# Loading the whole Toeplitz strip of a convolution from HBM in place of half of it

## The chip, the cores and the metric

The kernel runs on one core of a Trainium2 chip. The metric is the device time of one execution in microseconds (us), lower is better. All runs compared here are fast-state runs, each against runs of the kernel before on the same chip and in the same rounds. Experiments of different rounds are compared by their medians; the kernel before had medians of 2366.5 to 2369.3 us in all rounds. The Trainium skill, which is cited by page title below, is a set of notes on the chip; where a number below is not attributed to it, it comes from a run or a trace.

## The reference

```python
def _attn_ref(x, h) -> np.ndarray:       # x: (8, 5696, 128), h: (5696, 128), float32
    B, S, D = x.shape
    L = 2 * S
    Xf = np.fft.rfft(x, n=L, axis=1)
    Hf = np.fft.rfft(h, n=L, axis=0)
    Yf = Xf * Hf[None, :, :]
    y = np.fft.irfft(Yf, n=L, axis=1)[:, :S, :]
    return y.astype(np.float32)
# ... cut: a token- and channel-mixing layer on y follows, unchanged here
```

The first stage is a causal convolution along the sequence, with its own filter for each of the 128 channels.

## The kernel before

The convolution is done as matrix products. The sequence is cut into NT = 45 blocks of P = 128, and for channel `d` and block distance `k` TensorE needs the 128 x 128 Toeplitz block whose row p is the padded filter `h_pad[d]`, shifted by p elements. A *strip* holds KS = 15 such blocks side by side; its row p is 1920 neighbouring elements of `h_pad[d]`, starting at `j0 + p`. A channel takes three strips and 45 matmuls, which get narrower as `k` grows.

```python
x_sb2 = x_sb.rearrange("q d t b -> q d (t b)")
with tc.tile_pool(name="conv_sbuf", bufs=6) as csb, \
     tc.tile_pool(name="conv_psum", bufs=2, space=bass.MemoryType.PSUM) as cps:
    for d in range(D):
        psum = cps.tile([P, NT * B], F32, tag="convps")
        for k0 in range(0, NT, KS):
            k1 = k0 + KS
            w = KS * P
            j0 = P * k0
            strip = csb.tile([P, KS * P + 64], BF16, tag="strip")

            own, other, c0, c1 = ((slice(0, 64), slice(64, P), 0, 64) if d % 2 == 0 else
                                  (slice(64, P), slice(0, 64), 64, 0))
            nc.sync.dma_start(strip[own, :w + 64],
                              bass.AP(tensor=h_pad.tensor, offset=h_pad.offset + d * HW + j0,
                                      ap=[[1, 64], [1, w + 64]]))
            nc.vector.tensor_copy(strip[other, c0:c0 + w], strip[own, c1:c1 + w])
            for k in range(k0, k1):
                ntj = NT - k
                c = c0 + (k - k0) * P
                nc.tensor.matmul(psum[:, B * k: B * k + B * ntj],
                                 strip[:, c:c + P],
                                 x_sb2[:, d, :B * ntj],
                                 start=(k == 0), stop=(k == NT - 1))
        nc.scalar.activation(
            y_sb[:, :, :, d].rearrange("q t b -> q (t b)"), psum, AF.Copy)
# ... the mixing layer follows
```

Row p + 64 of a strip is row p shifted by 64 elements. So the DMA brings only 64 rows, 64 elements longer than needed, and VectorE copies them, shifted, into the other 64 partitions. Six buffers hold the strips, exactly two channels' worth.

Of the kernel before, what the change touches and what calls it, by code (L numbers as in the profile page):

```python
# [21 lines left out]
def kernel(  # L22
# [10 lines left out]
    nc = tc.nc  # L33
    B, S, D = x.shape
    assert D == 128
    P = 128
# [3 lines left out]
    HW = Sp + P  # L40
    KS = 15
# [12 lines left out]
    h_pad = h_pad_h.ap()  # L54
# [26 lines left out]
    with tc.tile_pool(name="s0", bufs=1, side="right") as s0, \  # L81
# [27 lines left out]
        for tj in range(NT):  # L109
            q_cnt = P if tj < NT - 1 else S_last  # L110
            tmp = xl.tile([P, B, D], F32, tag="xt")
            if q_cnt < P:
# [3 lines left out]
                                      ap=[[D, q_cnt], [S * D, B], [1, D]]))  # L116
# [22 lines left out]
# [7 lines that stand above are left out]
                j0 = P * k0  # L146
                strip = csb.tile([P, KS * P + 64], BF16, tag="strip")

                own, other, c0, c1 = ((slice(0, 64), slice(64, P), 0, 64) if d % 2 == 0 else
                                      (slice(64, P), slice(0, 64), 64, 0))  # L150
                nc.sync.dma_start(strip[own, :w + 64],
                                  bass.AP(tensor=h_pad.tensor, offset=h_pad.offset + d * HW + j0,
                                          ap=[[1, 64], [1, w + 64]]))
                nc.vector.tensor_copy(strip[other, c0:c0 + w], strip[own, c1:c1 + w])  # L154
                for k in range(k0, k1):
                    ntj = NT - k
                    c = c0 + (k - k0) * P
# [6 lines that stand above are left out]
# [148 lines left out]
    with tc.tile_pool(name="bpool", bufs=1, reuse_waits="tile") as bp, \  # L312
# [155 lines left out]
        for k, (p, tt, c) in enumerate(chunks):  # L468
            j0, nj = CHUNKS[c]
# [55 lines left out]
        for i, (k, p, tt, j0, s0, nj) in enumerate(stretches):  # L525
# [20 lines left out]
            if tt is None:  # L546
# [17 lines left out]
                if end_of_pair:  # L564
# [5 lines left out]
                    for h in range(2):  # L570
                        c, c0 = cs[h]
# [87 lines left out]
```

## Time and profile before

| | kernel before |
|---|---|
| time, median of 2 runs | 2368.76 us (2365.74 to 2371.78) |
| span of the profiled execution | 2367.9 us |
| convolution: first to last weight load | 106.7 to 597.9 us |
| a strip's DMA, issue to landing, median | 4.6 us |

The first view is that of one tile, `strip`, in the kernel before. The rows with a line number give an instruction group with its shortest, median and longest duration in ns and the first and last start in us. The indented rows with a tile's name say what ended the idle time of the engines that work on the tile (us in total, times); an indented `PEld` row comes from the view's second list, who waited for the tile, and is that of TensorE's weight loads alone.

```profile
L158 PEld LDWEIGHTS <-strip x5760: 95/98/152, 106.7 to 597.9; 128*128 128x128 bf16 x199
...
L151 SPq DMA_DIRECT2D strip<-h_pad x384: 444/445/1586, 100.8 to 590.4; - x192
L154 DVE COPY strip<-strip x384: 651/655/658, 106.0 to 595.3; 64x1920 bf16<-64x1920 bf16 x192
...
  DMA strip<-h_pad: 205.1, 309
  DVE strip L154: 36.8, 75
...
  PEld L158: 21.2, 41
...
DMA to landing us min/median/max: 3.3/4.6/7.2
```

The last weight load starts at 597.9 and the first at 106.7, so a strip takes (597.9 - 106.7) / 384 = 1.279 us. VectorE waits for strips (205 us), and TensorE waits for VectorE's copies.

The second is the view by stretches, of the kernel before, for 460 us within the convolution: the stretch and its length, busy us (and instructions) of TensorE, its weight loads, VectorE, ScalarE and GpSimd, then the granted clock, the busy share of the 16 DMA engines, and GB/s.

```profile
core 0: us, PE busy (x) PEld busy (x) DVE busy (x) ACT busy (x) POOL busy (x), PEclk, DMA share, GB/s
110.00:570.00 460.00, 445.47 (x5424) 382.55 (x5422) 235.10 (x361) 213.23 (x120) 0.00 (x0) 1.00 0.76 200
```

TensorE is busy 445 of 460 us at full clock, while the DMA engines are busy 76% at 200 GB/s. The third is the chain of waits of the kernel before, in order of time (start, us, what), a piece of the convolution.

```profile
215.71 5.75 PE psum L158 x60
...
221.48 5.27 DMA strip<-h_pad
...
226.87 0.67 DVE strip L154
...
227.58 13.09 PE psum L158 x150
...
240.68 4.76 DMA strip<-h_pad
```

Where TensorE waits for nothing it does 60 matmuls, four strips, in 5.75 us: a channel's three and the first and widest of the next channel, which takes 2.12 us. The three strips of a channel thus take 3.63 us, or 1.21 us a strip. Between such stretches the chain runs through a strip's DMA (about 5 us) and a copy (0.67 us).

### The profile page before, as it was taken

How to read it: one execution, taken by the hardware profiler on the slowest of the kernel's cores; microseconds unless marked ns; L12 is line 12 of the kernel's file. 1: busy time of each engine (PE TensorE's matmuls, PEld its weight loads, DVE VectorE, ACT ScalarE, POOL GpSimd, SP SyncE). 2: the span in 40 equal slices, each digit the busy share in tenths (PEclk: the TensorE clock that was granted, in tenths of full speed). 3: DMA queues.
4: the chain of work that ended last, by engine and by line, in shares of the span. 5: the costliest groups of instructions: out<-in, count | busy, mean ns of one | idle time of the engine just before them, and what ended most of it. 6: DMA issues, size and time to landing. Idle time of an engine off the chain costs nothing.

```text
span 2367.9 us, 39718 instructions
## 1 busy us (share of the span) xinstructions
PE 2191.0 (93%) x14513; PEld 1216.4 (51%) x14686; DVE 1649.6 (70%) x2997; ACT 639.2 (27%) x733; POOL 796.1 (34%) x1474
## 2 busy tenths in 40 slices
PE   4699999999666999999999999799999999999997
PEld 1188888888432444444444444234444444444443
DVE  5655555555577888887787776687677677677774
ACT  3544444444862333332232000001111111111111
POOL 0000000000201544544446564344544544544540
PEclk7599999999978999999999999899999999999998
DMA  9977777777998988988789997967877977977872
GB/s 238 251 204 203 200 204 202 202 197 202 232 284 218 164 156 168 164 165 156 134 168 164 159 151 128 286 101 134 156 136 130 160 134 134 160 132 136 151 135 54
DMA packets 435332, 405.51 MB, mean 171 GB/s; under 512 B 66497, under 2 KB 370625, under 8 KB 435009
## 3 DMA queue, kind: packets, MB, share of 16 engines
q0 software_dynamic: 222816, 131.33, 42.4%
q1 hardware_dynamic: 209296, 260.55, 38.9%
q10 hardware_dynamic: 3024, 11.08, 1.3%
q8 instruction: 116, 1.90, 0.3%
q14 instruction: 80, 0.65, 0.1%
HBM read 449.27 MB, written 84.75 MB: 226 GB/s over the span
## 4 chain that ended last, share of the span: by engine, by line
PE 70%; DMA 15%; DVE 8%; issue 3%; POOL 2%; ACT 1%; SPq 1%; DVEq 0%; ACTq 0%; POOLq 0%
PE m L598 51%; PE psum L158 14%; DMA strip<-h_pad 6%; DMA tmp<-in_x_dram 2%; DVE c L605 2%; POOL wb L326 2%; DMA wb<-in_moe_w_tok_r_dram 2%; DMA wb<-in_moe_w_tok_i_dram 2%; DMA h_bf<-in_h_dram 1%; DVE wt L335 1%; DVE strip L154 1%; PE v L419 1%; PE utp L412 1%; PE m L560 1%; PE m L562 1%
## 5 line engine op out<-in xcount | busy, mean ns | idle before, releaser
L326 POOL DMA_DIRECT2D wb<-in_moe_w_tok_i_dram x720 | 388.7, 547 | 801.7 <-DVE wt L335 713.8
L326 POOL DMA_DIRECT2D wb<-in_moe_w_tok_r_dram x720 | 387.6, 546 | 714.4 <-PE psum L158 594.3
L158 PE MATMUL psum<-x_sb,strip 128*128 128x360 bf16 (+44 forms) x5760 | 474.1, 243 | 17.0 <-DVE strip L154 15.2
L598 PE MATMUL m<-b,wt 128*128 128x512 bf16 x1892 | 453.7, 383 | 26.9 <-DVE wt L335 9.8
L158 PEld LDWEIGHTS <-strip 128*128 128x128 bf16 x5760 | 406.5, 98 | 85.4 <-DVE strip L154 21.2
L335 DVE STREAM_TRANSPOSE wt<-wb 128x384 f32<-128x384 f32 (+2 forms) x720 | 359.8, 524 | 123.1 <-PE m L598 73.5
L154 DVE COPY strip<-strip 64x1920 bf16<-64x1920 bf16 x384 | 250.7, 655 | 239.3 <-DMA strip<-h_pad 205.1
L598 PEld LDWEIGHTS <-wt 128*128 128x128 bf16 x1936 | 190.6, 99 | 259.8 <-issue 27.6
L162 ACT ACTIVATE y_sb<-psum 128x360 bf16<-128x360 f32 x128 | 227.4, 1777 | 264.4 <-PE psum L158 264.4
L605 DVE TENSOR_TENSOR c<-c,m 128x512 f32<-128x512 f32 x440 | 284.0, 671 | 0.0
L414 ACT ACTIVATE uts<-utp 128x512 bf16<-128x512 bf16 (+1 forms) x90 | 53.3, 592 | 616.7 <-PE utp L412 616.7
L409 ACT ACTIVATE ub<-c 128x512 bf16<-128x512 f32 (+1 forms) x90 | 56.5, 628 | 226.6 <-DVE c L605 226.3
L121 PE MATMUL rps<-tmpbf,R_bf 128*128 128x512 bf16 x88 | 45.7, 620 | 52.1 <-DVE tmpbf L118 52.0
L185 ACT ACTIVATE yT<-tpz 128x512 bf16<-128x512 bf16 x68 | 39.7, 596 | 191.5 <-PE tpz L181 191.5
L118 DVE CAST tmpbf<-tmp 128x1024 bf16<-128x1024 f32 x45 | 56.7, 1267 | 33.3 <-DMA tmp<-in_x_dram 33.1
L199 ACT ACTIVATE red<-theta_ps,magic 128x512 f32<-128x512 f32 x46 | 31.6, 687 | 151.3 <-PE theta_ps L197 116.9
L421 DVE SCALAR_TENSOR_TENSOR c<-v,c 128x512 f32<-128x512 f32 (+1 forms) x90 | 61.6, 684 | 11.3 <-PE v L419 10.8
L123 ACT ACTIVATE x_sb<-rps 128x1024 bf16<-128x1024 f32 x45 | 46.1, 1024 | 57.8 <-PE rps L121 50.1
L219 ACT ACTIVATE mag<-mag,half_pi 128x512 f32<-128x512 f32 (+1 forms) x68 | 57.8, 850 | 0.2
L605 DVE TENSOR_TENSOR c<-yy,m 128x512 f32<-128x512 bf16 x88 | 56.1, 679 | 0.9 <-PE m L598 0.9
L121 PEld LDWEIGHTS <-R_bf 128*128 128x128 bf16 x90 | 6.2, 111 | 89.5 <-DVE tmpbf L118 80.8
L217 ACT ACTIVATE mag<-red 128x512 f32<-128x512 f32 x46 | 29.0, 630 | 77.6 <-DVE red L201 77.6
(2759 smaller groups left out, 2967.7 us busy)
## 6 DMA issues: line engine op xcount, KB each, us to landing
strip<-h_pad SPq DMA_DIRECT2D x384, 248.0 KB, 4.6
wb<-in_moe_w_tok_r_dram POOLq DMA_DIRECT2D x352, 96.0 KB, 4.4
wb<-in_moe_w_tok_i_dram POOLq DMA_DIRECT2D x352, 96.0 KB, 4.6
wb<-in_moe_w_tok_r_dram POOLq DMA_DIRECT2D x352, 80.0 KB, 4.3
wb<-in_moe_w_tok_i_dram POOLq DMA_DIRECT2D x352, 80.0 KB, 3.7
tmp<-in_x_dram SPq DMA_DIRECT2D x44, 512.0 KB, 5.8
cp_hbm<-c SPq DMA_DIRECT2D x88, 256.0 KB, 2.5
c<-cp_hbm SPq DMA_DIRECT2D x88, 256.0 KB, 4.6
```

The lines of the kernel that those rows point to most:

```text
L118: nc.vector.tensor_copy(tmpbf, tmp.transpose([0, 2, 1]))
L154: nc.vector.tensor_copy(strip[other, c0:c0 + w], strip[own, c1:c1 + w])
L158: nc.tensor.matmul(psum[:, B * k: B * k + B * ntj], strip[:, c:c + P], x_sb2[:, d, :B * ntj], start=(k == 0), stop=(k == NT - 1))
L162: nc.scalar.activation(y_sb[:, :, :, d].rearrange("q t b -> q (t b)"), psum, AF.Copy)
L219: nc.scalar.activation(mag, mag, AF.Sin, bias=half_pi, scale=-TWO_PI)
L326: nc.gpsimd.dma_start(wb[32 * i:32 * i + 32, :ng, :nj * 64], bass.AP(tensor=a.tensor, offset=a.offset + row0 * S + p * H + i * QR + j0 * 6 ...
L335: nc.vector.transpose(wt.rearrange("p j t r -> p (j t r)").bitcast(F32).rearrange("p (j g t) -> p g j t", j=TJ, g=4)[:, :ng, :nj], wb[:, : ...
L409: nc.scalar.activation(ub[:m].rearrange("p b d -> p (b d)"), c[:m], AF.Copy)
L414: nc.scalar.activation(uts[:, :, :m], utp[:, :, :m], AF.Copy)
L421: nc.vector.scalar_tensor_tensor(c[:m], v[:m], 0.0, c[:m], op0=ALU.max, op1=ALU.add)
L598: nc.tensor.matmul(ms[q], a[q][:, j, :, r], bts[jj][q][:, r, :], start=(jj == 0 and r == 0), stop=(jj == NJ - 1 and r == 1 and q not in left))
L605: nc.vector.tensor_tensor(c, z, ms[q], op=op)
```

## The change

The intent is to free VectorE and to take its copy out of the way between DMA and TensorE: the DMA brings all 128 rows, and to carry twice the DMA work the strips are issued in turn on the sync and the scalar queue.

```diff
-                own, other, c0, c1 = ((slice(0, 64), slice(64, P), 0, 64) if d % 2 == 0 else
-                                      (slice(64, P), slice(0, 64), 64, 0))
-                nc.sync.dma_start(strip[own, :w + 64],
-                                  bass.AP(tensor=h_pad.tensor, offset=h_pad.offset + d * HW + j0,
-                                          ap=[[1, 64], [1, w + 64]]))
-                nc.vector.tensor_copy(strip[other, c0:c0 + w], strip[own, c1:c1 + w])
+                eng = nc.sync if (d * 3 + k0 // KS) % 2 == 0 else nc.scalar
+                c0 = 0
+                eng.dma_start(strip[:, :w],
+                              bass.AP(tensor=h_pad.tensor, offset=h_pad.offset + d * HW + j0,
+                                      ap=[[1, P], [1, w]]))
```

The number of buffers, six, and their width stay.

## The prediction

> **What bounds the kernel now.** The change touches only the convolution (106 to 598 us of a 2368 us span). By stretches, TensorE is busy 57 to 58.7 of every 60 us there at granted clock 1.00; the chain of waits shows one channel's three strips, back to back, in 3.63 us, so 128 channels need at least 465 us. About 490 pass. The other 25 us are waits: by the wait view TensorE sits idle 36 us for VectorE's half-strip copy (74 times), and VectorE 205 us for the strip's DMA (309 times). The chain alternates: TensorE frees a buffer, a strip lands about 5 us later, 0.66 us of copy, TensorE again. The stage is close to TensorE-bound; a loop of six buffers and slow strips just shows through. DMA is 73 to 78% busy, moving only 200 GB/s.
>
> **Why the strips are slow.** A strip fills 64 partitions. The Trainium skill, "SBUF — State Buffer", section "Door 1", says that partitions 0 to 63 reach only 8 of 16 DMA ports. The trace agrees: 3968-byte packets come in two groups, about 153 ns (40%) and about 310 ns, as if two engines shared a port.
>
> **What the change does.** Removes 384 VectorE copies (655 ns each; on the path only as latency). Doubles the strips' bytes: 128 rows of 3840 B instead of 64 of 3968, 189 MB instead of 98. Half of the DMAs move to ScalarE's queue; the same skill ("DMA: Bandwidth & Descriptors", "Issuing engines are not separate DMA queues") says that this gives no bandwidth. ScalarE's compiled order puts later strips between the evictions (1.78 us), two channels ahead, so a strip is issued at most about 1.8 us late; I expect that to be hidden. Matmuls and later stages are unchanged.
>
> **Sum.** Each of 16 engines moves 8 packets per strip. From the uncontended 153 ns for 3968 B: about 149 ns each, 1.21 us per strip with the semaphore write. From the 4096-byte, 128-partition b loads under full load (mean 172 ns, 370 to 380 GB/s): about 161 ns, 1.30 us per strip (estimates). TensorE takes 1.21 us per strip. So DMA would set the stage: 384 x 1.21 to 1.30 = 465 to 503 us, against 490. The copy's latency is gone, but the DMA limit takes back about what it cost. All 128 rows read nearly the same 4 KB of HBM at once; if that costs, a strip takes 1.4 us or more and the stage 540 us.
>
> I predict a convolution of about 502 us and a time of 2381 us, 8 in 10 between 2352 and 2435. Faster by over 2%: 0.03; within 2%: 0.77; slower by over 2%: 0.20.
>
> **What would show it.** (1) No VectorE work between 110 and 595 us. (2) DMA busy 95% or more there, 360 to 400 GB/s. (3) Strip packets mostly at 150 to 165 ns, without the group at 310. (4) TensorE's idle time ended by strip DMAs, 30 to 60 us in all. (5) Issue to landing of a strip 4 to 6 us. (6) After the convolution everything merely shifted.
>
> **What would make it wrong.** Overlapping reads of one 4 KB piece of HBM served slowly (packets of 200 ns and more: 600 us, slower by over 2%). ScalarE's queue issuing late, so that TensorE waits for odd channels' third strip although DMA is not full. Or packets so near 149 ns that DMA keeps up: 470 us, 2350 us in all.

## The result

The changed kernel took 2436.52 us (median of 2 runs, 2435.28 to 2437.75). It is slower: the ratio is 1.0284, with a 95% interval of 1.0262 to 1.0306. Ratios here are the mean time of one kernel's fast runs over that of the other's of the same rounds, so they are not quite the ratio of the medians that are quoted.

The same tile view, of the changed kernel:

```profile
L157 PEld LDWEIGHTS <-strip x5760: 95/98/151, 105.9 to 668.0; 128*128 128x128 bf16 x199
...
L151 SPq DMA_DIRECT2D strip<-h_pad x192: 319/320/606, 100.5 to 659.8; - x192
L151 ACTq DMA_DIRECT2D strip<-h_pad x192: 326/326/682, 103.2 to 660.3; - x192
...
  DMA strip<-h_pad: 170.1, 199
...
  PEld L157: 96.8, 107
...
DMA to landing us min/median/max: 3.8/6.8/9.6
```

VectorE's copies are gone, and so is TensorE's wait for them. In their place stand waits for the strips' DMA: 96.8 us of the weight loads, where they waited 21.2 us before. (The 170.1 us add the idle time of the weight loads and of the matmuls, which mostly wait at the same moments, as do the 36.8 us of the kernel before.) A strip takes (668.0 - 105.9) / 384 = 1.464 us in place of 1.279, and lands 6.8 us after its issue, not 4.6. The convolution is (668.0 - 105.9) - (597.9 - 106.7) = 71 us longer, while the profiled span is 65.6 us longer: the whole loss lies in this stage.

The stretch of 110 to 570 us, of the changed kernel, with the columns as before:

```profile
110.00:570.00 460.00, 397.61 (x4733) 329.65 (x4730) 0.00 (x0) 186.14 (x105) 0.00 (x0) 1.00 0.89 336
```

TensorE is busy 48 us less in the same 460. VectorE does nothing. The DMA engines move 336 GB/s, but they are busy only 89%: **the stage waits for DMA, and yet DMA is not full.** That is the puzzle. The chain of waits of the changed kernel shows it too:

```profile
193.17 6.85 DMA strip<-h_pad
...
200.06 1.37 PE psum L157 x15
...
201.46 6.80 DMA strip<-h_pad
...
208.31 1.37 PE psum L157 x15
...
209.71 7.32 DMA strip<-h_pad
...
217.07 3.81 PE psum L157 x45
...
220.91 7.33 DMA strip<-h_pad
```

TensorE's last matmul on a buffer releases it, the next strip for that buffer takes about 7 us, TensorE works off mostly one to four strips, and the chain goes through a DMA again.

How the DMA is loaded over the whole run is in the page's second part, 40 equal slices of the span each; of the kernel before (slices of 59.2 us):

```profile
DMA  9977777777998988988789997967877977977872
GB/s 238 251 204 203 200 204 202 202 197 202 232 284 218 164 156 168 164 165 156 134 168 164 159 151 128 286 101 134 156 136 130 160 134 134 160 132 136 151 135 54
```

and of the changed kernel (slices of 60.8 us), where the third to the eleventh slice are the convolution:

```profile
DMA  9988999988899789988889997988779779778872
GB/s 240 287 330 344 340 343 352 345 327 329 314 267 295 174 168 161 168 155 171 134 162 162 165 158 135 213 178 136 135 138 155 135 132 157 139 130 152 142 133 60
```

In the changed kernel's convolution the DMA digit goes between 8 and 9 (9 is 90% or more) at 314 to 352 GB/s, where the kernel before has 7 at about 200; after it the two rows look alike.

### The profile page after: what moved, and what is told of

Read it like the earlier page. It is cut to its first block, busy times and chain, and to the rows that moved or that the text cites. A ratio compares the mean times of both kernels' runs of the same rounds, so it can differ in the third digit from the quotient of the medians.

```text
span 2433.5 us, 38685 instructions
## 1 busy us (share of the span) xinstructions
PE 2207.2 (91%) x14686; PEld 1209.2 (50%) x14686; DVE 1398.6 (57%) x2613; ACT 638.5 (26%) x733; POOL 797.9 (33%) x1474
## 4 chain that ended last, share of the span: by engine, by line
PE 68%; DMA 22%; DVE 5%; issue 2%; ACT 1%; SPq 1%; POOL 1%; DVEq 0%; ACTq 0%; POOLq 0%
PE m L597 54%; DMA strip<-h_pad 14%; PE psum L157 9%; DMA tmp<-in_x_dram 2%; DMA wb<-in_moe_w_tok_r_dram 2%; DVE c L604 1%; DMA h_bf<-in_h_dram 1%; PE utp L411 1%; PE v L418 1%; PE m L559 1%; PE m L561 1%; PE m L601 1%; DMA b<-zi_hbm 1%; DMA wb<-in_moe_w_tok_i_dram 1%; POOL wb L325 1%
## 5 line engine op out<-in xcount | busy, mean ns | idle before, releaser
L157 PE MATMUL psum<-x_sb,strip 128*128 128x360 bf16 (+44 forms) x5760 | 484.8, 243 | 76.9 <-DMA strip<-h_pad 73.3
L157 PEld LDWEIGHTS <-strip 128*128 128x128 bf16 x5760 | 401.5, 98 | 161.0 <-DMA strip<-h_pad 96.8
L597 PE MATMUL m<-b,wt 128*128 128x512 bf16 x1936 | 458.8, 384 | 19.4 <-ACT red L217 7.8
```

The lines of the kernel that those rows point to most:

```text
L157: nc.tensor.matmul(psum[:, B * k: B * k + B * ntj], strip[:, c:c + P], x_sb2[:, d, :B * ntj], start=(k == 0), stop=(k == NT - 1))
L597: nc.tensor.matmul(ms[q], a[q][:, j, :, r], bts[jj][q][:, r, :], start=(jj == 0 and r == 0), stop=(jj == NJ - 1 and r == 1 and q not in left))
```

## The experiments

Four explanations stood after the result.

- **Late scalar queue.** ScalarE evicts each channel's PSUM, and strip DMAs stand behind the evictions in its order.
- **Two queues interleave.** Two strips on two queues share the 16 DMA engines, so the one that TensorE needs first lands with the next one.
- **Overlapping reads.** The 128 rows of a strip are nearly the same 4 KB of HBM, and some packets stall.
- **Too few buffers.** The strips in flight are too few to fill the DMA for the time that one strip needs.

All experiments ran with 3 rounds, so each has 4 runs of its own. Three read wrong data on purpose; all others give the correct result. Three kinds of numbers below are counted from the trace and are in no view. Packet times come from its packet records. The times from a buffer's release to the issue of its next DMA, from a landing to the first weight load on the strip and from there to its last matmul come from its instruction records. "First to last share" and the gaps between landings come from its landing records: a strip's DMA leaves 16 such events, one for each share, and the strip is complete with the last.

### One queue (e1)

```diff
-                eng = nc.sync if (d * 3 + k0 // KS) % 2 == 0 else nc.scalar
+                eng = nc.sync
```

> The changed kernel with all 384 strips on the sync queue. The changed kernel took 2436 us. Theory 'late scalar queue' (a strip issued behind an eviction comes late): 2370 to 2400 us, and TensorE's idle time before the strips' matmuls well under 170 us. Theories 'stalled packets' (reads of nearly the same HBM bytes stall now and then) and 'too few buffers' expect no gain: 2425 to 2450 us, as the same bytes go through the same 16 engines.

It took 2408.31 us (ratio 1.0179), 28 us less than the changed kernel: between the two expectations, so neither theory had the whole. Tile view and stretch:

```profile
L157 PEld LDWEIGHTS <-strip x5760: 95/98/152, 105.7 to 645.6; 128*128 128x128 bf16 x199
...
L151 SPq DMA_DIRECT2D strip<-h_pad x384: 319/320/1542, 100.1 to 637.9; - x192
...
  DMA strip<-h_pad: 120.7, 174
...
  PEld L157: 67.5, 92
...
DMA to landing us min/median/max: 3.8/6.6/9.8
```

```profile
110.00:570.00 460.00, 412.50 (x4912) 346.56 (x4911) 0.00 (x0) 193.14 (x109) 0.00 (x0) 0.99 0.91 349
```

The second queue cost 28 us of the 68 (e16 and e18 below, a pair from the same rounds, give 22). The other 40 remain with full strips on the queue of before. Which of the two explanations of the queue holds, this run does not tell.

### Evictions on VectorE, strips still on two queues (e8)

```diff
-            nc.scalar.activation(
-                y_sb[:, :, :, d].rearrange("q t b -> q (t b)"), psum, AF.Copy)
+            nc.vector.tensor_copy(
+                y_sb[:, :, :, d].rearrange("q t b -> q (t b)"), psum)
```

> The changed kernel with the eviction of each channel's PSUM on VectorE, which is idle in this stage, so the strip DMAs of the scalar queue stand behind nothing. Theory 'late scalar queue': as fast as one queue (2400 to 2412 us). Theory 'two queues interleave on each DMA engine': 2430 to 2440 us, like the changed kernel, and the strips still land in pairs.

It took 2439.55 us (ratio 1.0309). Tile view:

```profile
  DMA strip<-h_pad: 167.1, 214
...
  DVE y_sb L161: 341.5, 128
...
DMA to landing us min/median/max: 3.6/6.8/9.2
```

The scalar queue now has no evictions in front of its strips (VectorE, which now evicts, waits for the PSUM instead: the row of 341.5 us, from the list of those who waited), and nothing is gained. The traces agree: in the changed kernel and here a strip's DMA is issued a median 0.03 us after the end of the last matmul that used the buffer, or 0.04 us on the scalar queue. The late scalar queue is refuted.

The landing records show what two queues do. With two, a strip often lands together with the one before it; with one, never:

| kernel | gaps between successive landings under 0.6 us | over 2.5 us | first to last share of a strip, mean |
|---|---|---|---|
| changed (two queues) | 111 of 357 | 65 | 2.69 us |
| e8 (two queues, no evictions there) | 109 of 356 | 64 | 2.65 us |
| e1 (one queue) | 0 of 357 | 22 | 2.28 us |

The Trainium skill, "DMA: Bandwidth & Descriptors", section "Queues, rings and completion order", says that a DMA engine goes round robin between the queue rows it has work for. Landing in pairs agrees with that: the strip that TensorE needs would share the engines with the next one, and neither is early. Counted over the stage, a strip lands a mean 6.74 us after its issue with two queues and 6.54 us with one (e1), and then lies 0.56 us, against 0.38, before TensorE takes it. That interleaving is the cause is what is left when the late queue is refuted; no run shows it directly.

### The queue part of the change alone (e7)

```diff
-                nc.sync.dma_start(strip[own, :w + 64],
+                (nc.sync if (d * 3 + k0 // KS) % 2 == 0 else nc.scalar).dma_start(strip[own, :w + 64],
```

on the kernel before.

> The queue part of the change alone: the kernel before with its half strips in turn on the sync and the scalar queue. Theory 'two queues interleave strips and so delay the one that TensorE waits for' and theory 'late scalar queue': slower by 5 to 30 us (2375 to 2400), as with full strips, where one queue was 28 us faster than two. If the queue part only hurts where DMA is full: 2363 to 2375.

It took 2367.34 us (ratio 1.0007, interval 0.9990 to 1.0023): no effect. A second queue costs where DMA is nearly full, not at 200 GB/s.

### Rows that share no bytes (e2, e3, e12)

```diff
-                              bass.AP(tensor=h_pad.tensor, offset=h_pad.offset + d * HW + j0,
-                                      ap=[[1, P], [1, w]]))
+                              bass.AP(tensor=h_pad.tensor, offset=h_pad.offset + j0,
+                                      ap=[[HW, P], [1, w]]))      # e2; e3 has HW + 1
```

Both are edits of the changed kernel; e12 is e2 on the sync queue alone.

> Wrong result on purpose: each of the 128 partitions reads its own row of h_pad (rows 11776 bytes apart, 256-byte aligned), so no two rows of a strip share HBM bytes; bytes, descriptors, queues and buffers as in the changed kernel. Theory 'stalled packets from overlapping reads': packets over 0.3 us nearly vanish (they are 2.5% in the changed kernel), the strips move at over 390 GB/s, convolution 475 to 490 us, 2345 to 2365 us in all. Theory 'too few buffers': 2425 to 2445 us, as nothing in the buffer loop changes.

> As the run before it, but each row starts 2 bytes further along, so the starts are unaligned as in the changed kernel while no bytes are shared. If overlap is the cause it is as fast as the aligned one (within 10 us). If alignment is the cause it is as slow as the changed kernel, 2436 us.

> Wrong result on purpose: own row of h_pad for each partition (nothing shared), all on one queue. With two queues own rows gained 32 us on the changed kernel and one queue gained 28 us. If the two are separate causes: 2370 to 2385 us. If both only even out the same unevenness: 2400 to 2410 us, as each of them alone. If overlap as such costs nothing on one queue, equal to the one-queue run, 2408 us.

They took 2404.91 us (e2), 2403.96 us (e3) and 2381.88 us (e12); all three are wrong. Of e2, the stretch of 110 to 570 us:

```profile
110.00:570.00 460.00, 421.95 (x5014) 348.21 (x5013) 0.00 (x0) 196.71 (x111) 0.00 (x0) 1.00 0.98 358
```

The edit also drops the channel from the address, so every channel reads the same three sets of rows; what it gains may belong to that as well. Neither expectation of e2 was met: it gained 32 us, between the "all" of one theory and the "nothing" of the other. Alignment makes no difference (e2 against e3). The stalled-packet story in the form in which it was put is wrong: packets over 0.3 us did not vanish but rose from 2.5% to 3.3%. What changed is that the DMA engines are busy 98% and not 89%. On one queue the same edit gained 26 us (e1 to e12), so the queue and the reads are separate costs. Why the overlapping rows of the change leave engines idle more often is not settled; the experiments below show that overlap as such does not cap the rate.

### Shorter strips in more buffers (e4, e9, e10)

```diff
-    KS = 15
+    KS = 9                                   # e4, e9; e10: 5
-    with tc.tile_pool(name="conv_sbuf", bufs=6) as csb, \
+    with tc.tile_pool(name="conv_sbuf", bufs=10) as csb, \      # e4, e9; e10: 20
-                strip = csb.tile([P, KS * P + 64], BF16, tag="strip")
+                strip = csb.tile([P, KS * P], BF16, tag="strip")
```

e4 keeps two queues, e9 and e10 use the sync queue alone.

> Correct result. Strips of 9 blocks in 10 buffers in place of 15 blocks in 6, nearly the same SBUF bytes; 640 DMAs of 2304-byte rows. TensorE holds a tenth of the ring and not a sixth, so more is in flight. Theory 'too few buffers': convolution 525 us or less (from 563), 2390 to 2405 us in all. Theory 'stalled packets' alone: about 10 to 25 us gained at the most, as the stalls stay. If the fixed cost of each DMA counts: as slow as the changed kernel or slower.

> Both remedies on the changed kernel: strips of 9 blocks in 10 buffers, all on the sync queue. Two queues cost 28 us with long strips; short strips gained 50 us. If the two causes are independent: 2360 to 2370 us, level with the kernel before. If finer strips already repair what two queues spoil: 2378 to 2388 us, as with short strips on two queues.

> Strips of 5 blocks in 20 buffers, one queue: 1152 DMAs of 1280-byte rows. With 9 blocks the DMA moved 384 GB/s, its engines always busy, and the time was 2372 us. If only the bytes at that rate are left to pay, this stays at 2365 to 2380 us; if shorter rows cost more per byte (93 ns for 2304 bytes against 149 ns for 3840: about 8 ns each are fixed), the DMA takes 20 to 30 us more: 2385 to 2405 us.

e4 took 2386.02 us, 50 us less than the changed kernel: a little better than the buffer theory expected, and twice what stalls alone allowed. e9 took 2372.37 us, 36 us less than e1 and 2 us above the range for independent causes. In e9 the DMA is full at last: busy share 1.03 at 384 GB/s between 110 and 570 us. (The view adds packet times, so the share can pass 1.)

e10 missed by far, at 2532.89 us, and shows a limit of its own. Its 20 buffers are not used: TensorE frees a buffer a median 6.2 us before the DMA for it is issued, and the issue comes a median 0.08 us after the landing of the *eighth* DMA before it. The compiled order says why: each DMA gets one of eight completion semaphores in turn and waits until the one before on it is done. Eight strips of 160 KB in flight are less than is needed, and the DMA stays at 286 GB/s. The same limit is at work in e4 and e9, which the expectations did not see: there too the issue comes a median 0.08 and 0.06 us after the landing of the eighth DMA before it, so their ten buffers hold at most eight strips in flight.

### One buffer more (e11), and its confound (e16, e19)

```diff
-    with tc.tile_pool(name="conv_sbuf", bufs=6) as csb, \
+    with tc.tile_pool(name="conv_sbuf", bufs=7) as csb, \
-                strip = csb.tile([P, KS * P + 64], BF16, tag="strip")
+                strip = csb.tile([P, KS * P], BF16, tag="strip")
```

on top of e1. The 64 unused columns had to go for a seventh buffer to fit.

> Full strips of 15 blocks on the sync queue with one buffer more (7; the tile loses its 64 unused columns). Only the number of buffers differs from the one-queue run with 6 (2408 us). If the ring of six buffers is what the uneven landing of a strip's 16 shares runs into: 2375 to 2395 us. If the DMA's rate alone limits: unchanged, 2402 to 2412 us.

It took 2350.50 us (ratio 0.9923): 58 us less than e1, more than expected, and faster than the kernel before. Tile view and stretch of e11:

```profile
L157 PEld LDWEIGHTS <-strip x5760: 95/98/151, 105.9 to 581.5; 128*128 128x128 bf16 x199
...
L151 SPq DMA_DIRECT2D strip<-h_pad x384: 319/320/1360, 100.1 to 574.0; - x192
...
  DMA strip<-h_pad: 9.6, 22
...
  PEld L157: 5.7, 13
...
DMA to landing us min/median/max: 3.4/6.5/10.1
```

```profile
110.00:570.00 460.00, 455.55 (x5601) 393.97 (x5600) 0.00 (x0) 219.72 (x124) 0.00 (x0) 1.00 1.01 399
```

TensorE's weight loads wait 5.7 us for strips, where e1 had 67.5. The DMA is full, at 399 GB/s, with the overlapping reads of the change and not a byte less to move. Packets over 0.3 us, which had looked like a cause, fell from 1.8% to 0.5%, so they are no fixed price of overlapping reads. The run changed two things, however: a buffer more, and a buffer size that is a multiple of 256 bytes. Two runs separate them: e16 has six buffers of 3840 bytes, e19 seven of 3904.

> The one-queue kernel (2408 us, six buffers of 3968 bytes a partition) with the tile's 64 unused columns cut off: six buffers of 3840 bytes, each now at a 256-byte boundary. The seven-buffer run (2350 us) changed both the number and this size. If the seventh buffer made its gain: 2402 to 2412 us here, unchanged. If where the rows start in SBUF made it: 2350 to 2365 us.

> The reverse: seven buffers on one queue, but of 3904 bytes a partition, so that the buffers start off 256-byte boundaries (3968 does not fit seven times). If the seventh buffer is the cause: 2348 to 2360 us, as with 3840 bytes. If the start of the rows is: 2395 to 2412 us, and packets over 0.3 us come back (1.8% with six wide buffers, 0.5% with seven narrow ones).

e16 took 2413.28 us and e19 2350.26 us. The gain is the seventh buffer's; the size of the buffers, and with it where their rows start, does not matter.

### Seven buffers with two queues (e18, e17)

e18 is the changed kernel with the narrower tile only, e17 has the narrower tile and seven buffers.

> The changed kernel with nothing altered but the tile's 64 unused columns, which are cut off (buffers at 256-byte boundaries). Seventh-buffer theory: 2430 to 2440 us, unchanged. Row-start theory: 2360 to 2385 us.

> The changed kernel, two queues kept, with seven buffers of 3840 bytes. If two queues cost by letting strips share the DMA engines, a slower landing that a longer ring can hide: 2352 to 2375 us, most of the 28 us that two queues cost with six buffers gone. If two queues cost DMA rate: 2375 to 2400 us.

e18 took 2435.54 us, unchanged. e17, the change exactly as it was meant plus one buffer, took 2366.51 us (ratio 0.9992, interval 0.9973 to 1.0010): **one buffer takes back the whole loss.** Of its tile view:

```profile
L157 PEld LDWEIGHTS <-strip x5760: 95/98/152, 106.2 to 597.8; 128*128 128x128 bf16 x199
...
DMA to landing us min/median/max: 3.7/6.9/9.1
```

A strip still takes 6.9 us to land, but TensorE is done with the stage at 597.8 us and not at 668.0. It still is 16 us behind one queue (e19, same rounds). With six buffers two queues cost 22 us (e16 to e18, same rounds) or 28 us (e1 to the changed kernel). The runs of one of these kernels spread over up to 13 us, so whether the longer ring hides a part of this cost is not clear.

### Five buffers (e20, e21)

```diff
-    with tc.tile_pool(name="conv_sbuf", bufs=6) as csb, \
+    with tc.tile_pool(name="conv_sbuf", bufs=5) as csb, \
```

on e1 (e20) and on the kernel before (e21).

> Full strips on one queue with five buffers (six: 2408 us, seven: 2350). In the traces a strip's DMA is issued 0.03 us after TensorE frees the buffer, so the rate is buffers divided by a buffer's round trip, which with six is 6 x 1.397 = 8.4 us. If that round trip is latency and stays: 1.68 us a strip, 645 us of convolution, about 2510 us. If it is mostly queueing behind other strips it shrinks with the ring: 2420 to 2460 us.

> The kernel before with five buffers in place of six. Its round trip is 6 x 1.276 = 7.7 us. If it too is bound by the ring, with a round trip that stays: 1.53 us a strip, 588 us of convolution, about 2465 us. If six buffers were enough for half strips and TensorE sets the pace: 2368 to 2385 us.

e20 took 2504.21 us, as the constant round trip expected. e21 took 2419.72 us, between its two expectations. Tile view of e20:

```profile
L157 PEld LDWEIGHTS <-strip x5760: 95/98/152, 105.8 to 740.2; 128*128 128x128 bf16 x199
...
  DMA strip<-h_pad: 247.0, 219
...
  PEld L157: 131.4, 117
...
DMA to landing us min/median/max: 3.2/6.2/8.6
```

With one strip less in flight a strip still takes a median 6.2 us to land, although the DMA is now busy only 84% of the time. The table puts the ring together. "Us per strip" is the time from the first to the last weight load over 384, and the round trip of a buffer is that times the number of buffers. Both are of the profiled execution, which in e1 and e20 was the slowest of the four (2416.8 and 2512.1 us). The parts are means counted from the trace: issue to landing, landing to the first weight load on the strip (with half strips VectorE's copy lies in it), and from there to the end of its last matmul. They add up to the round trip within 0.2 us, so it is measured, and not only the rate turned round.

| kernel | strips, queues | buffers | us per strip | round trip, us | of it landing, lying, in use, us | time, us |
|---|---|---|---|---|---|---|
| e20 | full, one | 5 | 1.652 | 8.3 | 6.05, 0.65, 1.50 | 2504 |
| e1 | full, one | 6 | 1.406 | 8.4 | 6.54, 0.38, 1.41 | 2408 |
| e11 | full, one | 7 | 1.239 | 8.7 | 6.66, 0.50, 1.42 | 2350 |
| changed | full, two | 6 | 1.464 | 8.8 | 6.74, 0.56, 1.41 | 2437 |
| e17 | full, two | 7 | 1.280 | 9.0 | 6.87, 0.52, 1.42 | 2367 |
| e21 | half, one | 5 | 1.419 | 7.1 | 4.24, 1.34, 1.43 | 2420 |
| before | half, one | 6 | 1.279 | 7.7 | 4.60, 1.54, 1.42 | 2369 |

Full strips have a round trip of 8.3 to 9 us, whatever the number of buffers. (In e11 TensorE nearly sets the pace, and a landed strip lies a median 0.69 us before its first use; in e1 the median is 0.14 us.) TensorE uses a strip in 1.21 us, so a ring of six gives it 7.26 us and a ring of seven 8.47 us. Full strips do not fit into the first and just fit into the second. Half strips turned round in 7.1 us in e21, so six buffers just held them, with no slack for jitter: the kernel before pays about 25 us over TensorE's 465.

### The half strips, in the other order (e5, e15)

```diff
-                own, other, c0, c1 = ((slice(0, 64), slice(64, P), 0, 64) if d % 2 == 0 else
+                own, other, c0, c1 = ((slice(0, 64), slice(64, P), 0, 64) if (d * 3 + k0 // KS) % 2 == 0 else
```

on the kernel before; e15 has strips of 9 blocks in 10 buffers besides (and `d * 5`).

> The kernel before (half strips, VectorE makes the other half), but the half that the DMA fills alternates with each strip and not with each channel, so strips that follow each other use opposite partition halves. If 64 partitions share 8 of 16 ports, neighbours in flight no longer collide: the packets' group at 310 ns shrinks, landing falls from 4.6 us to about 4, the convolution from 492 to about 475 us: 2345 to 2360 us. If the ports were not what slowed them: 2363 to 2373, unchanged.

> The best so far (half strips whose half alternates with each strip, 2352 us), with strips of 9 blocks in 10 buffers. TensorE waits there only some 11 us for VectorE in all, and needs 465 us: if shorter strips and more of them in flight take these waits away, 2340 to 2350 us; if the 256 more copies and DMAs cost as much as they bring, 2348 to 2362 us.

e5 took 2351.89 us (ratio 0.9946) and e15 2347.13 us (ratio 0.9899, interval 0.9873 to 0.9926), the fastest of all. Tile view of e5:

```profile
L158 PEld LDWEIGHTS <-strip x5760: 95/98/152, 106.3 to 581.8; 128*128 128x128 bf16 x199
...
  DVE strip L154: 11.1, 31
...
DMA to landing us min/median/max: 3.2/4.2/6.8
```

Strips in flight one after the other now fill opposite halves of the partitions. The part of their packets that took over 0.3 us fell from 27% to 12%, landing from 4.6 to 4.2 us, and the row of TensorE's wait for VectorE from 36.8 to 11.1 us (its weight loads alone: from 21.2 to 7.3). In e15 TensorE never waits in the stretch that was looked at:

```profile
110.00:570.00 460.00, 460.00 (x5695) 399.09 (x5694) 286.27 (x630) 223.78 (x126) 0.00 (x0) 1.00 0.66 215
```

## Why the prediction was wrong

The prediction was 2381 us, in a range of 2352 to 2435, with "within 2%" the most likely. The result, 2436.5 us, lies just outside the range, and slower by more than 2%, which had a chance of 0.20.

**What held.** The bound before was read rightly: TensorE with a loop of six buffers just showing through; only the 36 us of idle TensorE are the doubled row, 21 us of weight loads. The port reading agrees with the runs: packets over 0.3 us fell from 27% to 2.5% with full strips, and alternating the halves (e5) gained what it should. Two clean groups of packets there are not in the kernel before: 32% took 150 to 160 ns, 27% over 300 ns, and the rest lay between. The estimates of a packet held: the median was 149 ns and the mean 162 ns, against 149 and 161. VectorE's work is gone, the wait moved to the strips' DMA, the scalar queue's order did no harm (e8), and later stages merely shifted, to within 6 us.

**The step that failed** is "So DMA would set the stage: 384 x 1.21 to 1.30". The rate as such was right: e11, with the same bytes, takes 1.239 us a strip. What was wrong is that the DMA would be kept full. It was expected busy 95% or more at 360 to 400 GB/s, and was busy 89% at 336. TensorE's idle time was put at 30 to 60 us, and its weight loads waited 97 us for strips. The prediction named the loop of six buffers in its first paragraph and then left it out of the sum. A strip's landing was put at 4 to 6 us and took a mean 6.7; with 0.6 us until TensorE takes the strip and 1.4 us in use that makes a buffer's round trip 8.7 us by its parts (8.8 by the rate), and six buffers over 8.8 us give 1.46 us a strip. The term that sets the stage was that quotient, not the DMA's rate. That one buffer more restores the time of before (e17) shows it.

**The second failing** is about the queues. The prediction said that a second queue "gives no bandwidth" and counted it as free. It gives none, and it is not free: 22 to 28 us with six buffers, 16 us with seven, nothing with half strips. Strips land in pairs with it; that it costs by this is an inference.

**A named risk that was half right.** Overlapping reads were feared as packets of 200 ns and more. The median packet stayed at 149 ns, but rows without overlap, which every channel read again, gained 26 to 33 us with six buffers (e2, e3, e12). How overlap leaves the DMA engines idle stays open. Open too is why a full strip, whose bytes need 1.2 us, takes over 6 us to land even with five buffers; uneven shares (2.1 us from the first to the last in e20) may be a part of it, and queueing is: in e20 a strip landed after a mean 4.5 us when one other was in flight at its issue, 5.5 with two, 6.0 with three and 6.7 with four. That is about 0.7 us for each strip ahead and leaves some 3.8 us that no other strip explains (an estimate from these four means); no run isolates what they are.

## What to carry to other kernels

Where a ring of buffers feeds an engine, the rate is the number of buffers over the time for which one buffer is taken (from its release through the transfer to the end of its use), and that has to be computed beside each engine's and the DMA's own rate. Larger transfers lengthen that time (7.1 to 7.7 us with half strips here, 8.3 to 9 us with full ones), so a ring that just sufficed for half the bytes may fail with all of them, while the DMA shows as not quite full; try one buffer more before anything else. Put transfers that are needed in order on one queue when DMA is nearly full.

## What the Trainium skill lacked or had wrong

- "DMA: Bandwidth & Descriptors", section "Issuing engines are not separate DMA queues": it says that a second issuing engine only saves issue time. It lacks that it can cost: in order on one queue against in turn on two was 2408 against 2437 us here (2413 against 2436 in the narrower pair), with 111 of 357 strips landing within 0.6 us of the one before in place of none.
- "SBUF — State Buffer", section "The DMA setup-cost knee": 2 us fixed plus 436 GB/s make 3.1 us for a full strip of 491,520 bytes (an estimate from that page). The shortest landing in a trace was 3.2 us (e20), which agrees; but the median in a running ring was 6.2 to 6.9 us. No page gives a rule for the number of buffers from the landing time in a loaded ring.
- "SBUF — State Buffer", section "Door 1": that 64 partitions reach half of the ports agrees with the trace (peaks of the packet times at about 153 and about 310 ns in the kernel before). Its section "Can I just issue two DMAs to hit both halves?" calls such DMAs serialized, at +6% over one. Here, alternating the halves from strip to strip shortened the landing from 4.6 to 4.2 us and the kernel from 2366 to 2352 us, so it is worth doing where a strip's latency counts.
- "DMA: Bandwidth & Descriptors", section "Where 436 GB/s comes from": it lets about 358 GB/s bind between HBM and SBUF. That is too broad: elsewhere the same page gives about 358 GB/s for each of two cores that stream at once, and 408.7 GB/s for one alone. With one core at work, e11 moved 399 GB/s over 460 us, with reads that overlap almost wholly.
- No page has that DMAs wait for the landing of the eighth before them when eight completion semaphores are used in turn, which is how this kernel was compiled: with strips of 160 KB that held the DMA at 286 GB/s (e10).
